# Mixture-of-experts kernel: weight maxima spread by one bf16 product, two experts without transposed results, one slot reordering moved

## The chip, the cores and the metric

The program runs on one core of a Trainium2 chip. Its engines are TensorE (PE, with its weight loads PEld), VectorE (DVE), ScalarE (ACT), GpSimd (POOL) and SyncE (SP, which issues transfers); each works through its own queue in order. The metric is the device time of one execution in microseconds (us).

## The reference

Attention over 4 batches of 768 tokens with 8 heads of 64, each query seeing the last 96 keys and 8 global ones, then a mixture of 8 experts of which each token uses two:

```
a = softmax(scale * q k^T + bias, masked);  x = a v           # x: 3072 tokens x 512
noisy = x @ w_gate + log1p(exp(x @ w_noise)) * noise
top2  = the two largest of 8 per token, weights = softmax of the two
for e in range(8):  out[tokens of e] += weight * (relu(x[tokens] @ w1[e]) @ w2[e])
```

Here w1[e] is 512 x 1024 and w2[e] is 1024 x 512, everything in float32.

## The kernel before

The first part (about 186 us) is attention, with gating and routing woven in. After it the experts run one after the other. An expert has a fixed number of slots, `CAPS`: 812 for the first three places, then 788, 776, 772, and 768 for places 6 and 7. The first two places hold experts 0 and 1; the other experts are put into places 2 to 7 by the number of their tokens (`rank`). The slots are split into a first part of 512 (four tiles of 128, `TA`) and the rest (300 down to 256, up to three tiles).

Products are done in three fp16 passes: every weight and activation is split into a high and a low half (`w1h`, `w1l`, `w2h`, `w2l`, `hh`, `hl`). To split the weights, each matrix needs one power-of-two scale, for which its largest magnitude must be known on all partitions. `scales` (line 156) does that, in six steps: four reductions `wmx` of 128x1024 on DVE (L162), then a PE transpose of the four columns (L166), a DVE maximum over them (L168) and a small diagonal (L170), and in the next step an fp32 product with ones (L173) and a maximum over its four columns (L175). It runs 16 times, twice for each expert. `step(e)` calls the next step of the preparation of expert e: these six, then eight `split`s, for W1 and then for W2. A table in the expert loop says how many steps follow which block of PE work; that order is what each engine's queue gets.

An expert's blocks on PE are:

- `up(e, 0, f)`, eight of twelve matmuls with 512 columns (L914), then `up(e, 1, f)`, eight on the rest of the slots. ACT writes `hh` (L924), DVE writes `hl` (L925).
- `down(e, t)`, four blocks of 24 matmuls with 512 columns (L947), one for each tile of the first part; the slots are the stationary operand, so the result has a slot on each partition and `put` writes it out (L931 on ACT, an adding indirect DMA on POOL, L932).
- `down_t(e, d)`, four blocks of 24 matmuls (L958) for the rest, with the weights stationary and 256 to 300 slots as columns. The result is transposed (`yt`, copied by ACT at L963 and DVE at L961), and `back` (L969) turns each tile round with four fp32 PE transposes before `put`. For all experts but the last this is done within the next expert's `up` blocks.

Between the blocks the next expert's token rows are gathered (POOL, L270), split (`ready`, `rest`: DVE L286 to L303, ACT L290) and transposed by DMA (`turn`). `permute(a, z)` (line 252) reorders the slot lists of places a to z-1 on DVE (L255, L257) and writes them as integers to `ids` (L258), which the gathers of these places read. `permute(2, 4)` stands after the sixth `up` block of expert 0's rest; `gather(2, ...)` follows in the third `up` block of expert 1.

Of the kernel before, what the change touches and what calls it, by code (L numbers as in the profile page):

```python
# [10 lines left out]
F32 = mybir.dt.float32  # L11
# [9 lines left out]
P = 128  # L21
# [15 lines left out]
def tile_local_global_attention_then_moe(  # L37
# [43 lines left out]
    def bank(tag, bufs):  # L81
        return psum.tile([P, 512], F32, name=tag, tag=tag, bufs=bufs)
# [26 lines left out]
    row = consts.tile([P, P], F16, name="row")  # L109
    col = consts.tile([P, E * (TT + 1)], F16, name="col")  # L110
    over = consts.tile([P, NT, E], F32, name="over")
    wmx = consts.tile([P, E, 2, 4], F32, name="wmx")
    wex = consts.tile([P, E, 2], F32, name="wex")
    wsc = consts.tile([P, E, 2], F32, name="wsc")
    fac = consts.tile([P, E], F32, name="fac")
    up2 = consts.tile([P, 2], F32, name="up2")
    one4 = consts.tile([4, P], F32, name="one4")
    noise_s = consts.tile([P, NT, E], F32, name="noise_s")
    wgn = consts.tile([P, KC, 32], F32, name="wgn")
    sel = consts.tile([P, 2 * E], F32, name="sel")  # L120
# [35 lines left out]
    def scales(e, x):  # L156

        m, c = wmx[:, e, x - 1], slice(x - 1, x)
        for i in range(4):
            t = raw[x, e, i // 2].rearrange("p k f -> p (k f)")  # L160
            n = t.shape[1] // 2
            nc.vector.tensor_reduce(m[:, i:i + 1], t[:, i % 2 * n:(i % 2 + 1) * n], op=OP.max, axis=AX.X,  # L162
                                    apply_absolute_value=True)
            yield
        ps = bank("sc", 3)
        nc.tensor.transpose(ps[:4, :P], m, ident)  # L166
        mc = small.tile([4, 1], F32, name="mc")
        nc.vector.tensor_reduce(mc, ps[:4, :P], op=OP.max, axis=AX.X)  # L168
        d4 = small.tile([4, 4], F32, name="d4")
        nc.vector.tensor_scalar(d4, ident[:4, :4], mc, TINY, op0=OP.mult, op1=OP.max)  # L170
        yield
        ps = bank("sc", 3)
        nc.tensor.matmul(ps[:, :4], one4, d4, start=True, stop=True)  # L173
        m1 = small.tile([P, 1], F32, name="m1")
        nc.vector.tensor_reduce(m1, ps[:, :4], op=OP.max, axis=AX.X)  # L175
        power(wex[:, e, c], m1, wsc[:, e, c])
        nc.vector.tensor_mul(wsc[:, e, c], wsc[:, e, c], up2[:, c])
        if x == 2:
            nc.vector.scalar_tensor_tensor(fac[:, e:e + 1], wex[:, e, 0:1], 2.0 ** -(1 + W1_UP + W2_UP),
                                           wex[:, e, 1:2], op0=OP.mult, op1=OP.mult)  # L180
        yield
# [20 lines left out]
    def weigh(e, a, z):  # L202
        c = l1[:, e, a:z]
        nc.vector.tensor_scalar(c.bitcast(I32), c.bitcast(I32), EXP, None, op0=OP.bitwise_and)
        nc.vector.scalar_tensor_tensor(yr[:, e, a:z], wv[:, e, a:z], fac[:, e:e + 1], c, op0=OP.mult, op1=OP.mult)
# [46 lines left out]
    def permute(a, z):  # L252
        for e in range(a, z):
            m = small.tile([P, TT, E], F32, name="m78")
            nc.vector.tensor_mul(m, flat[:, :, :TT].rearrange("p e t -> p t e"),  # L255
                                 pick[:, e, None, :].to_broadcast([P, TT, E]))
            nc.vector.tensor_reduce(flat2[:, e, :TT], m, op=OP.add, axis=AX.X)  # L257
        nc.vector.tensor_copy(ids[:, a:z, :TT], flat2[:, a:z, :TT])  # L258
# [237 lines left out]
    with ExitStack() as actx:  # L496
# [102 lines left out]

        def gate_consts():  # L600
            nc.vector.tensor_copy(ident16, ident)
            nc.vector.memset(one4, 1.0)
            nc.vector.memset(up2[:, 0:1], 2.0 ** (W1_UP - 1))
            nc.vector.memset(up2[:, 1:2], 2.0 ** (W2_UP - 1))
            nc.vector.memset(wgn, 0.0)
            nc.sync.dma_start(wgn[:, :, :2 * E], w_gn.rearrange("(k p) e -> p k e", p=P))
            nc.vector.tensor_add(sel, ident[:, 0:2 * E], ident[:, 32:32 + 2 * E])
            nc.vector.tensor_add(sel, sel, ident[:, 64:64 + 2 * E])
            nc.vector.tensor_add(sel, sel, ident[:, 96:96 + 2 * E])
# [287 lines left out]
    with ExitStack() as mctx:  # L897
# [42 lines left out]

        def down(e, t):
            ps = bank("av", 2)
            cols = slice(t * P, (t + 1) * P)
            n = 0
            for f in range(FC):
                for x, w in ((hh, w2h), (hh, w2l), (hl, w2h)):
                    nc.tensor.matmul(ps, x[0][:, f, cols], w[e % 2][:, f], start=n == 0, stop=n == 3 * FC - 1)  # L947
                    n += 1
            put(e, t, ps)

# [73 lines left out]
        for f in range(FC):  # L1024
            up(0, 1, f)
            if f in (0, 2, 4):
                rest(1, 1 + f // 2)
                turn(1, 1 + f // 2)
            if f in (0, 2):
                ready(1, 2 + f // 2)  # L1030
            if f in (0, 3):
                load_w()
            if f not in (0, 2):
                step(1)
            if f == 1:
                rank()
            if f == 5:
                permute(2, 4)
        ready(1, TA)
        for j in range(KC):  # L1040
            down_t(0, j)
            step(1)
            if j < TB:
                rest(1, TA + j)
                turn(1, TA + j)
                if j + 1 < TB:
                    ready(1, TA + j + 1)
        weigh(0, TA, TT)
        for e in range(1, E):
            last = e + 1 == E  # L1050
            for f in range(FC):
                up(e, 0, f)
                if f < tiles(e - 1) - TA:
                    back(e - 1, f)
                step(e, [0, 0, 0, 1, 0, 1, 2, 2][f])
                if f == 2 and not last:
                    for t in range(5):
                        gather(e + 1, t)
            weigh(e, 0, tiles(e))
            if e == 1:  # L1060
                permute(4, E)
                limits()
            for f in range(FC):
                up(e, 1, f)
                if f < 2:
                    step(e, 2)
                elif f < 6:
                    step(e + 1)
                if not last:
                    if f in (4, 6):  # L1070
                        ready(e + 1, f // 2 - 2)
                    if f in (5, 7):
                        rest(e + 1, f // 2 - 2)
                        turn(e + 1, f // 2 - 2)
                        if f // 2 + 3 < tiles(e + 1):
                            gather(e + 1, f // 2 + 3)
            steps = [(down, t) for t in range(TA)]
            steps_t = [(down_t, d) for d in range(KC)]
            for j, (f, t) in enumerate(steps_t + steps if last else steps + steps_t):
                f(e, t)  # L1080
                if not last:
                    if j < tiles(e + 1) - 2:
                        ready(e + 1, j + 2)
                    step(e + 1, [1, 3, 3, 3, 1, 1, 1, 1][j])
                    if j < tiles(e + 1) - 2:
                        rest(e + 1, j + 2)
                        turn(e + 1, j + 2)
                elif KC <= j < KC + tiles(e) - TA:
                    back(e, j - KC)


# [85 lines left out]
```

## Time and profile before

| | us |
|---|---|
| median of 3 runs | 738.0 (736.62 to 739.31) |
| span of the profiled execution | 738.1 |
| PE busy | 703.6 (95%) |
| DVE busy | 491.7 (67%) |
| ACT busy | 343.3 (47%) |
| POOL busy | 203.2 (28%) |

The page gives the profiled execution no time of its own beside its span, from the first to the last instruction. A matmul's printed length holds its way through the array and overlaps the next one, so the pace is read from start to start. In square brackets stands how long the engine was idle before an instruction, and what ended that.

### The profile page before, as it was taken

What the parts mean: (1) busy time and instruction counts of PE and PEld (TensorE: products, weight loads), DVE (VectorE), ACT (ScalarE), POOL (GpSimd) and SP (SyncE); (2) the same over time, 40 slices, a digit from 0 to 9 for tenths busy, and PEclk for the clock granted to TensorE, in tenths of its full rate; (3) what the DMA queues carried; (4) which work ended last, traced back from release to release, by engine and by line L of the source; (5) the groups of instructions that cost most, each with busy time, mean ns of one, the idle gap of its engine ahead of it and who ended that gap; (6) DMA issues with size and microseconds to landing.
All of it is one profiled execution on the core that took longest, in us unless ns stands there. A gap on an engine that the chain in (4) does not pass through costs nothing. (4 is left out here: it accounts for less than half of the span.)

```text
span 738.1 us, 16394 instructions
## 1 busy us (share of the span) xinstructions
PE 703.6 (95%) x6191; PEld 449.0 (61%) x6191; DVE 491.7 (67%) x1714; ACT 343.3 (47%) x740; POOL 203.2 (28%) x205
## 2 busy tenths in 40 slices
PE   7999988896999899999999999999999999999996
PEld 5888767675445665565646465655656475665762
DVE  6668996978688746873767386658837754873600
ACT  5887776666344424252443345243424434342511
POOL 2100185130337532224131504132240314121013
PEclk9999998999899999999999999999999999999999
DMA  7889794656608974395559538745954774472015
GB/s 222 254 275 286 231 316 133 224 187 244 243 6 161 215 151 135 106 199 88 168 101 177 106 121 143 143 105 153 172 113 149 113 169 92 105 111 28 1 18 74
DMA packets 105544, 111.43 MB, mean 151 GB/s; under 512 B 51332, under 2 KB 64340, under 8 KB 105456
## 3 DMA queue, kind: packets, MB, share of 16 engines
q1 hardware_dynamic: 93408, 83.89, 41.7%
q0 software_dynamic: 11504, 26.15, 20.2%
q8 instruction: 51, 0.84, 0.5%
q14 instruction: 37, 0.30, 0.1%
q10 hardware_dynamic: 544, 0.26, 0.1%
HBM read 71.22 MB, written 27.71 MB: 134 GB/s over the span
## 5 line engine op out<-in xcount | busy, mean ns | idle before, releaser
L932 POOL DMA_INDIRECT out_dram<-y,ids x54 | 85.7, 1587 | 210.1 <-ACT y L931 206.5
L914 PEld LDWEIGHTS <-w1h 128*128 128x128 f16 x1024 | 99.8, 98 | 64.5 <-issue 1.7
L914 PE MATMUL at<-xx,w1h 128*128 128x512 f16 (+5 forms) x512 | 124.7, 334 | 0.2 <-DVE hl L925 0.2
L914 PE MATMUL sc<-xx,w1h 128*128 128x512 f16 (+5 forms) x512 | 122.8, 330 | 0.0
L270 POOL DMA_INDIRECT xg<-xd,ids x54 | 55.4, 1026 | 159.4 <-DVE hl L925 86.0
L947 PE MATMUL av<-w2h,hh 128*128 128x512 f16 x256 | 97.1, 379 | 0.0
L947 PE MATMUL av<-w2l,hh 128*128 128x512 f16 x256 | 97.1, 379 | 0.0
L947 PE MATMUL av<-w2h,hl 128*128 128x512 f16 x256 | 97.1, 379 | 0.0
L682 ACT ACTIVATE a<-ns,mx 128x168 f32<-128x168 f32 (+1 forms) x192 | 69.6, 421 | 42.3 <-DVE mx L679 41.4
L914 PE MATMUL at<-xx,w1l 128*128 128x512 f16 (+5 forms) x256 | 85.3, 333 | 0.0
L914 PE MATMUL sc<-xx,w1l 128*128 128x512 f16 (+5 forms) x256 | 84.5, 330 | 0.0
L947 PEld LDWEIGHTS <-hh 128*128 128x128 f16 x512 | 49.5, 98 | 56.0
L925 DVE SCALAR_TENSOR_TENSOR hl<-sc,hh 128x512 f16<-128x512 f32 (+5 forms) x63 | 35.5, 564 | 66.4 <-ACT hh L924 66.4
L162 DVE TENSOR_REDUCE wmx<-raw 128x1 f32<-128x1024 f32 x64 | 76.5, 1207 | 0.0
L290 ACT ACTIVATE xp<-xg,up 128x512 f16<-128x512 f32 x48 | 34.6, 721 | 89.0 <-DVE up L288 75.7
L958 PE MATMUL av<-hl,w2h 128*128 128x300 f16 (+4 forms) x256 | 72.5, 283 | 2.5 <-DVE hl L925 2.5
L958 PE MATMUL av<-hh,w2h 128*128 128x300 f16 (+4 forms) x256 | 72.6, 284 | 1.0 <-DVE yt L961 1.0
L958 PE MATMUL av<-hh,w2l 128*128 128x300 f16 (+4 forms) x256 | 72.4, 283 | 0.0
L914 PEld LDWEIGHTS <-w1l 128*128 128x128 f16 x512 | 50.3, 98 | 35.6 <-issue 0.7
L924 ACT ACTIVATE hh<-at 128x512 f16<-128x512 f32 (+5 forms) x62 | 30.5, 491 | 88.7 <-PE at L914 88.7
L925 DVE SCALAR_TENSOR_TENSOR hl<-at,hh 128x512 f16<-128x512 f32 (+5 forms) x62 | 34.8, 560 | 51.7 <-ACT hh L924 51.7
L720 PE MATMUL av<-vs,at 128*64 128x65 f32 (+1 forms) x768 | 60.0, 233 | 0.0
(194 smaller groups left out, 1239.1 us busy)
## 6 DMA issues: line engine op xcount, KB each, us to landing
raw<-in_w SPq DMA_DIRECT2D x32, 1024.0 KB, 7.4
out_dram<-zero SPq DMA_DIRECT2D x14, 512.0 KB, 5.8
vs<-in_v SPq DMA_DIRECT2D x24, 260.0 KB, 3.9
xd<-xr SPq DMA_DIRECT2D x24, 256.0 KB, 6.4
qs<-in_q SPq DMA_DIRECT2D x23, 256.0 KB, 6.1
ks<-in_k SPq DMA_DIRECT2D x19, 272.0 KB, 6.6
vp<-in_v SPq DMA_DIRECT2D x20, 195.0 KB, 4.6
ks<-in_k SPq DMA_DIRECT2D x4, 464.0 KB, 4.8
```

The costliest lines, as they stand in the source:

```text
L162: nc.vector.tensor_reduce(m[:, i:i + 1], t[:, i % 2 * n:(i % 2 + 1) * n], op=OP.max, axis=AX.X, apply_absolute_value=True)
L270: nc.gpsimd.indirect_dma_start(out=xg[e, t], out_offset=None, in_=xd[:n], in_offset=bass.IndirectOffsetOnAxis(ap=rows(e, t), axis=0), boun ...
L290: nc.scalar.activation(y[:m, :Dm], x[:, :Dm], AF.Copy, scale=u)
L682: nc.scalar.activation(A[m][:, s * w:(s + 1) * w], ns[:, s, :w], AF.Exp, bias=mx[:, s:s + 1], scale=-1.0)
L720: nc.tensor.matmul(ps[y * Q:(y + 1) * Q, h % 4], w, t, start=id(x) in first, stop=id(x) in final, tile_position=(r, y * Q))
L914: nc.tensor.matmul(ps, w[e % 2][:, k, fs], xx[c][:, x + k, :z], start=n == 0, stop=n == 3 * KC - 1)
L924: nc.scalar.activation(hh[c][:, f, :z], ps, AF.Relu)
L925: nc.vector.scalar_tensor_tensor(hl[c][:, f, :z], ps, 0.0, hh[c][:, f, :z], op0=OP.max, op1=OP.subtract)
L932: ins = nc.gpsimd.indirect_dma_start(out=out, out_offset=bass.IndirectOffsetOnAxis(ap=rows(e, t), axis=0), in_=y, in_offset=None, bounds_c ...
L947: nc.tensor.matmul(ps, x[0][:, f, cols], w[e % 2][:, f], start=n == 0, stop=n == 3 * FC - 1)
L958: nc.tensor.matmul(ps, w[e % 2][:, f, cols], x[1][:, f, :z], start=n == 0, stop=n == 3 * FC - 1)
```

## The change

Three things. First, the spreading of the maxima: DVE takes the maximum over the four columns on each partition (with a fifth column that holds a tiny constant), keeps only its exponent, and multiplies the identity matrix by it into a bf16 diagonal `dm` of 128x128; one bf16 product with ones puts all 128 values on every partition, and DVE takes the maximum over them. The transpose and the fp32 product go. Second, an expert whose rest is a multiple of 128 (places 6 and 7) runs `down` for all six tiles, without `down_t`, `yt` and `back`; the table of steps for it has six entries instead of eight. Third, `permute(2, 4)` stands after expert 0's last `down_t` block and `weigh`.

```diff
-    wmx = consts.tile([P, E, 2, 4], F32, name="wmx")
+    wmx = consts.tile([P, E, 2, 5], F32, name="wmx")
-    one4 = consts.tile([4, P], F32, name="one4")
...
+        m1 = small.tile([P, 1], F32, name="m1")
+        nc.vector.tensor_reduce(m1, m, op=OP.max, axis=AX.X)
+        nc.vector.tensor_scalar(m1.bitcast(I32), m1.bitcast(I32), EXP, None, op0=OP.bitwise_and)
+        d = small.tile([P, P], BF, name="dm")
+        nc.vector.tensor_scalar(d, ident, m1, None, op0=OP.mult)
+        yield
         ps = bank("sc", 3)
-        nc.tensor.transpose(ps[:4, :P], m, ident)
-        mc = small.tile([4, 1], F32, name="mc")
-        nc.vector.tensor_reduce(mc, ps[:4, :P], op=OP.max, axis=AX.X)
-        d4 = small.tile([4, 4], F32, name="d4")
-        nc.vector.tensor_scalar(d4, ident[:4, :4], mc, TINY, op0=OP.mult, op1=OP.max)
-        yield
-        ps = bank("sc", 3)
-        nc.tensor.matmul(ps[:, :4], one4, d4, start=True, stop=True)
+        nc.tensor.matmul(ps[:, :P], ones, d, start=True, stop=True)
         m1 = small.tile([P, 1], F32, name="m1")
-        nc.vector.tensor_reduce(m1, ps[:, :4], op=OP.max, axis=AX.X)
+        nc.vector.tensor_reduce(m1, ps[:, :P], op=OP.max, axis=AX.X)
...
-            nc.vector.memset(one4, 1.0)
+            nc.vector.memset(wmx[:, :, :, 4:], TINY)
...
         def down(e, t):
             ps = bank("av", 2)
-            cols = slice(t * P, (t + 1) * P)
+            c = t // TA
+            cols = slice((t - c * TA) * P, (t - c * TA + 1) * P)
...
-                    nc.tensor.matmul(ps, x[0][:, f, cols], w[e % 2][:, f], start=n == 0, stop=n == 3 * FC - 1)
+                    nc.tensor.matmul(ps, x[c][:, f, cols], w[e % 2][:, f], start=n == 0, stop=n == 3 * FC - 1)
...
-            if f == 5:
-                permute(2, 4)
...
         weigh(0, TA, TT)
+        permute(2, 4)
...
-                if f < tiles(e - 1) - TA:
+                if f < tiles(e - 1) - TA and (CAPS[e - 1] - CA) % P:
                     back(e - 1, f)
...
+            straight = (CAPS[e] - CA) % P == 0
...
-            steps = [(down, t) for t in range(TA)]
-            steps_t = [(down_t, d) for d in range(KC)]
+            steps = [(down, t) for t in range(tiles(e) if straight else TA)]
+            steps_t = [] if straight else [(down_t, d) for d in range(KC)]
...
-                    step(e + 1, [1, 3, 3, 3, 1, 1, 1, 1][j])
+                    step(e + 1, ([1, 3, 3, 3, 2, 2] if straight else [1, 3, 3, 3, 1, 1, 1, 1])[j])
...
-                elif KC <= j < KC + tiles(e) - TA:
+                elif not straight and KC <= j < KC + tiles(e) - TA:
                     back(e, j - KC)
```

On PE, between the first three `down` blocks of expert 6, where W1 of expert 7 gets its scale, there stood:

```order
L947 LDWEIGHTS hl_4134
L947 MATMUL av<-w2h_4126,hl_4134 128x512
L166 MATMUL sc<-ident,wmx 4x128
L947 LDWEIGHTS hh_4132
...
L947 MATMUL av<-w2h_4126,hl_4134 128x512
L173 MATMUL sc<-d_8901,one_103 128x4
L947 LDWEIGHTS hh_4132
```

and now, at the second of the two points alone:

```order
L946 MATMUL av<-w2h_4123,hl_4131 128x512
L171 LDWEIGHTS ones
L171 MATMUL sc<-dm,ones 128x128
L946 LDWEIGHTS hh_4129
L946 MATMUL av<-w2h_4123,hh_4129 128x512
```

The transpose of `wmx` is gone, and the product with ones stands where the fp32 one stood. On DVE the two rows `mc` and `d` become three (`m` twice, `dm`) at the same place of its queue.

On DVE, at the end of expert 0's `up` blocks for its rest (`hl` of the sixth, seventh and eighth block; `m`, `flat` and `ids` are `permute`), there stood:

```order
L297 SCALAR_TENSOR_TENSOR xp<-xg,up,xp 128x512
L925 SCALAR_TENSOR_TENSOR hl_4135<-sc,hh_4133 128x300
L255 TENSOR_TENSOR m_4949<-flat,pick 128x56
L257 TENSOR_REDUCE flat_86<-m_4949 128x7
L255 TENSOR_TENSOR m_4952<-flat,pick 128x56
L257 TENSOR_REDUCE flat_86<-m_4952 128x7
L258 CAST ids<-flat_86 128x2x7
L925 SCALAR_TENSOR_TENSOR hl_4135<-at,hh_4133 128x300
L925 SCALAR_TENSOR_TENSOR hl_4135<-sc,hh_4133 128x300
```

and now, with the five rows behind the last `yt` copy, the fourth `wmx` and `weigh`:

```order
L923 SCALAR_TENSOR_TENSOR hl_4132<-sc,hh_4130 128x300
L923 SCALAR_TENSOR_TENSOR hl_4132<-at,hh_4130 128x300
L923 SCALAR_TENSOR_TENSOR hl_4132<-sc,hh_4130 128x300
...
L203 SCALAR_TENSOR_TENSOR yr<-wv,fac,l_79 128x3
L253 TENSOR_TENSOR m_5119<-flat,pick 128x56
L255 TENSOR_REDUCE flat_86<-m_5119 128x7
L253 TENSOR_TENSOR m_5122<-flat,pick 128x56
L255 TENSOR_REDUCE flat_86<-m_5122 128x7
L256 CAST ids<-flat_86 128x2x7
L923 SCALAR_TENSOR_TENSOR hl_4131<-at,hh_4129 128x512
```

The last two `hl` of expert 0 follow the one before them directly, and the five rows stand ahead of the first `hl` of expert 1.

On ACT, at the end of expert 6 and the start of expert 7, there stood:

```order
L216 ACTIVATE w1h_114<-raw,wsc 128x4x128 x3
L963 ACTIVATE yt<-av 128x256 x2
L924 ACTIVATE hh_4132<-at 128x512
L931 ACTIVATE y<-sc,yr 128x512
L924 ACTIVATE hh_4132<-sc 128x512
L931 ACTIVATE y<-lg,yr 128x512
```

and now:

```order
L214 ACTIVATE w1h_113<-raw,wsc 128x4x128 x3
L929 ACTIVATE y<-av,yr 128x512 x2
L922 ACTIVATE hh_4129<-at 128x512
L922 ACTIVATE hh_4129<-sc 128x512
```

The two results `y` of the rest come straight from the product's bank, ahead of expert 7's blocks.

## Rows read from the trace of the kernel before

**Rows 1.** The page's first line.
```profile
span 738.1 us, 16394 instructions
```
**Rows 2.** Stretch of experts 1 to 7: us, busy (instructions) by engine, granted clock, DMA.
```profile
265.10:730.60 465.50, 463.82 (x2817) 276.02 (x2815) 282.66 (x637) 178.82 (x319) 118.36 (x89) 1.00 0.58 117
```
**Rows 3.** Order of time, PE, expert 6's first `down` blocks: start, us, instruction.
```profile
639.38 0.27 PE L166 MATMUL sc<-ident,wmx 128*4 128x128 f32 x1
639.49 0.38 PE L947 MATMUL av<-w2h,hh 128*128 128x512 f16 x1
...
644.45 0.38 PE L947 MATMUL av<-w2h,hl 128*128 128x512 f16 x1
644.76 0.38 PE L173 MATMUL sc<-d,one 4*128 4x4 f32 x2
645.07 0.39 PE L947 MATMUL av<-w2h,hh 128*128 128x512 f16 x1
```
**Rows 4.** Order of time, PE, fp16 transposes of 128 columns.
```profile
229.68 0.62 PE L317 MATMUL sc<-ident,xp 128*128 128x128 f16 x8
230.14 0.61 PE L317 MATMUL lg<-ident,xp 128*128 128x128 f16 x8
```
**Rows 5.** DVE by line and shape: count, busy us, mean ns, idle before.
```profile
L168 DVE TENSOR_REDUCE mc<-sc 4x1 f32<-4x128 f32 x16 | 4.3, 270 | 0.4 <-PE sc L166 0.4
L170 DVE TENSOR_SCALAR d<-ident,mc 4x4 f32<-4x4 f32 x16 | 4.0, 253 | 0.6
L175 DVE TENSOR_REDUCE m<-sc 128x1 f32<-128x4 f32 x16 | 2.4, 152 | 0.0
...
L601 DVE CAST ident<-ident 128x128 f16<-128x128 f32 x1 | 0.2, 222 | 0.0
```
**Rows 6.** Who waited for whom, PE: total us, times, longest us.
```profile
PE av L958 <- DVE yt L961: 1.0, 3, 0.6
```
**Rows 7.** Order of time, expert 4's `down` blocks into `down_t`, DVE and PE.
```profile
521.57 2.08 DVE L221 SCALAR_TENSOR_TENSOR w1l<-raw,wsc,w1h 128x512 f16<-128x512 f32 x3 [1.45 <-ACT w1h L216]
...
533.38 0.27 PE L958 MATMUL av<-hh,w2h 128*128 128x264 f16 x1 [0.64 <-DVE yt L961]
```
**Rows 8.** Order of time, expert 3, POOL and DVE at a scale.
```profile
445.69 0.94 POOL L270 DMA_INDIRECT xg<-xd,ids  x1 [2.88 <-issue]
...
446.20 0.22 DVE L170 TENSOR_SCALAR d<-ident,mc 4x4 f32<-4x4 f32 x1
```
**Rows 9.** Order of time, around `permute(2, 4)`, all engines.
```profile
251.41 0.42 ACT L924 ACTIVATE hh<-sc 128x300 f16<-128x300 f32 x1
...
251.51 0.29 PE L958 MATMUL av<-hl,w2h 128*128 128x300 f16 x1 [0.83 <-DVE hl L925]
...
253.72 0.41 PE L958 MATMUL av<-hl,w2h 128*128 128x300 f16 x1 [1.66 <-DVE hl L925]
```
**Rows 10.** Stretches, columns as in rows 2 (a POOL column too), granted clock third from the end.
```profile
179.60:185.30 5.70, 3.25 (x70) 2.65 (x70) 4.62 (x19) 3.34 (x8) 0.00 (x0) 1.00 0.27 102
...
250.20:253.60 3.40, 1.02 (x7) 0.52 (x6) 3.26 (x10) 2.25 (x5) 3.32 (x3) 1.00 0.38 62
253.60:257.00 3.40, 3.28 (x14) 1.98 (x14) 3.33 (x9) 1.03 (x2) 3.24 (x3) 0.50 1.00 373
```
**Rows 11.** Order of time, PE, expert 6's `down_t` blocks and a `back`.
```profile
655.44 0.27 PE L958 MATMUL av<-hh,w2h 128*128 128x256 f16 x1
...
665.92 0.59 PE L914 MATMUL at<-xx,w1h 128*128 128x512 f16 x2
...
668.51 0.60 PE L969 MATMUL sc<-ident,yt 128*128 128x128 f32 x4
668.95 0.59 PE L914 MATMUL sc<-xx,w1h 128*128 128x512 f16 x2
```
**Rows 12.** Order of time, attention, W2 of expert 0: PE and DVE.
```profile
129.75 0.27 PE L166 MATMUL sc<-ident,wmx 128*4 128x128 f32 x1 [2.02 <-DVE sli L450]
...
132.40 0.16 DVE L725 TENSOR_SCALAR den<-av 128x4 f32<-128x4 f32 x1 [0.85 <-PE av L720]
```

## The prediction

> **What bounds the kernel now.** I read the page's head for the span, 738.1 us [rows 1], then the busy time by stretch. In the stretch of experts 1 to 7, 63% of the span, PE is busy 463.82 of 465.50 us at a granted clock of 1.00, DVE 282.66, ACT 178.82 [rows 2]. The reader is to see that PE has no room there: a PE instruction that goes shortens the span by its own pace, unless another engine then ends the block. Third, PE in order of time at the instructions that go [rows 3, 11], for their pace from start to start. Fourth, the list of who PE waited for [rows 6] and the places of its longest waits [rows 7, 9, 12], since what PE saves ahead of a wait on another engine comes back as a longer wait.
>
> The runs have a median of 738.0 us, 0.1 under the profiled span; I work from 738.1.
>
> **The maxima, PE's part.** Expert matmuls with 512 columns follow each other by 0.216 us: from 639.49 to 644.45 there are 23 of them in 4.96 us [rows 3]. The transpose takes 639.38 to 639.49, 0.11 us. The fp32 product takes more: from the start of the last matmul before it, 644.45, to that of the first one after it, 645.07, are 0.62 us, where 0.216 would pass without it, so 0.40 us. Together 0.51 us go for each scale.
>
> The new product has 128 columns of 16 bits with a weight load ahead of it. Nothing in the trace is just that. The nearest is eight transposes of 128 fp16 columns, each with a weight load of its own: 229.68 to 230.14, 0.057 us each [rows 4]. A bound above is 0.40, what the fp32 product costs; below it is nothing. I take 0.06, the row that agrees with it in columns and width. That leaves 0.45 saved at each scale. There are 14 within the experts' work (two each for experts 1 to 7): 6.3 us. The two of expert 0 lie in attention and come below.
>
> **The maxima, DVE's part.** Before: L168 0.27, L170 0.25, L175 0.15, sum 0.67 us. After: a maximum over five columns and a mask, each about like L175 (0.15), the diagonal, nearest a cast of 128x128 fp32 to 16 bits (L601, 0.22), and a maximum over 128 values in PSUM, nearest L168 with as many for each partition (0.27): 0.79 us [rows 5]. So DVE has 0.12 us more for each scale; its own waits for the transpose go.
>
> In most places that is hidden behind PE. It is not in the `down` blocks, where DVE and ACT work in turns: DVE waits for ACT's `w1h` 1.45 us before its three `w1l` in expert 4, ACT having waited for DVE's row scales before. At the end of that chain stands DVE's `yt` copy, and PE waits for its bank 0.64 us [rows 7]. There are three such waits, 1.0 us in all [rows 6]. In these three experts PE comes 0.45 us earlier and the chain ends 0.12 us later, so the wait can grow by up to 0.57 us: 1.7 us in all, or nothing if the chain starts from PE's `down` results after all. I take 1.3, near the upper end, because the wait that is shown in front of the chain's longest step is for ACT and not for PE. Left of this part: 6.3 - 1.3 = 5.0 us.
>
> **The slots of places 2 and 3.** At 251.51 PE waits 0.83 us for the sixth `hl` of expert 0, and at 253.72 another 1.66 us for the seventh, which on DVE stands behind the five rows of `permute` [rows 9]. The first wait stays, since that `hl` stands ahead of `permute` before and after. The second goes, down to what the eighth `hl` needs: ACT has its `hh` at 251.41 + 0.42 = 251.83 us [rows 9], and DVE follows; I leave 0.1 for that. So 1.55 us.
>
> In the 3.4 us of these two waits PE was busy 1.02 us, and the granted clock then fell to 0.50, the 1.2 GHz level, for 3.4 us, in which 14 matmuls started [rows 10]; at 2.4 GHz they take half of that, so the fall cost some 1.6 us. With the second wait gone PE is idle about 1 us there. In attention PE was busy 3.25 of 5.70 us from 179.60 on and the clock stayed at 1.00 all that time [rows 10]. So I take it that the clock holds, 1.6 us; the other end is nothing. Sum 3.15 us.
>
> What the step issues where it now stands: five DVE instructions, about 1.3 us, no transfer of its own. Behind them on DVE waits the first `hl` of expert 1, which nobody needs before that expert's `down`, and its bank is wanted two blocks of 2.6 us later. The gathers of place 2 stand on POOL behind three `put`s of expert 0, which come with expert 1's first three blocks, so `ids` is in time. Cost nothing; if the cover were gone, at most the 1.3 us. SP's queue keeps its order.
>
> **The two straight experts.** `down_t` in expert 6 takes 655.44 to 665.92, 10.48 us for 96 matmuls [rows 11]. Instead there are 48 with 512 columns at 0.216, 10.35. Each `back` takes four fp32 transposes, 668.51 to 668.95, 0.44 us [rows 11], and there are two for each expert. So 0.13 + 0.88 = 1.0 us, twice: 2.0 us. DVE and ACT lose the `yt` copies. The two `put`s come earlier, and the last instructions of the program, a `down` block, its `y` and its transfer, are of the same kind and size as before.
>
> **Attention.** At 129.75 PE has waited 2.02 us at the transpose, whose PSUM bank DVE still reads, and DVE in turn waits 0.85 us for PE's `av` at 132.40 [rows 12]. Without the transpose PE goes on, but DVE has little idle time there, so the gain is what DVE waited, 0.85, less its 0.12. Ends: the whole 2.02 plus 0.9 for the PE time of the two scales, and a loss of 0.5 if DVE's added work falls where it sets the pace. I take 0.7.
>
> **Sum.** 5.0 + 3.15 + 2.0 + 0.7 = 10.85, so 738.1 - 10.85 = 727.2 us.
>
> **Rivals.**
> 1. *Nothing is given back.* If the `yt` chain hangs on PE's results, its 1.3 us are saved, and attention may give up to 2 us more: 724 us. For it: ACT's `y` in the same blocks does wait for PE. Against it: the three waits are there now.
> 2. *The clock falls again.* After the wait that stays at 251.51, or at the longer `yt` wait of expert 4 (0.64 + 0.57 = 1.2 us). Each costs 1.6: 728.8 or 730.4 us. Against it: the stretch from 179.60.
> 3. *POOL holds up the diagonal.* At 446.20 the small diagonal ran 0.22 us inside a POOL gather of 0.94 us [rows 8], unhindered. The 128x128 one may not be: if it waits out such a gather, 0.7 us more come into the chain in the `down` blocks of six experts, 4.2 us, 731.4 us. The Trainium skill, page "SBUF — State Buffer", section "Who interferes with whom", says that a `tensor_scalar` in a two-port mode and a GpSimd instruction shut each other out for a whole instruction, whoever comes first. By that rule the 0.22 us row should have ended only with the gather, so the trace does not bear it out for the 4x4 form; no run here shows the 128x128 form.
> 4. *The product isn't cheap.* If the bf16 product costs PE the 0.40 us of the fp32 one, 14 x 0.34 = 4.8 us go: 732.0 us. Then the change would not do what it says. Against it: the fp16 transposes.
> 5. *Slower.* Rival 3, and in each of those `down` blocks the longer wait takes the clock down too, 1.6 us each. With n of them 731.4 + 1.6 n; from five on (739.4) it is slower than before, with six 741.0 us. Against it: no wait for `yt` has done that so far.
>
> **How the numbers follow.** Forecast 55% (own range 725.5 to 729), rival 1 17%, rival 2 14%, rival 3 7%, rival 4 4%, rival 5 3%. The range leaves out rivals 4 and 5, most of 3, and what runs scatter: 723.0 to 731.0 us. A difference of 0.3%, 2.2 us, is about what a measurement tells from no change. All cases but rival 5 are more than that below 738.0; for mishaps in two parts at once I allow some: faster 0.93, same 0.04, slower 0.03.
>
> **What would show it.** Right: L173's successor 0.06 us long from start to start, with no matmul behind it late; the PE wait for `hl` near 251 us once, under 1.2 us, and no half clock after it; no `down_t` in the last two experts, whose time from the first `down` block on is 1 us shorter; PE's waits for `yt` longer, 2.3 us in three places. Wrong: a wait of PE for `dm`, a `dm` of over 0.5 us beside POOL, a half clock in the experts, or attention longer than 186 us.

## The result, and the profile after

The changed kernel takes 730.06 us (median of four runs, 729.51 to 730.3) where the kernel before takes 738.57 in the same set (736.62 to 739.31): ratio 0.9878, 95% interval 0.9846 to 0.9910, so 8.5 us less. The forecast was 10.85 less, 727.2 us, with a range of 723.0 to 731.0. Two further sets of runs, on chips 14 and 12 (the chip of the first set is not on record), gave 0.9842 (0.9813 to 0.9871) and 0.9876 (0.9852 to 0.9901), 11.5 and 9.2 us less. What is the same in all of them, and what differs, is the matter of the experiments.

One thing on the scale first: a run's time lies 1.7 to 1.8 us above its span (730.3 against 728.5 for the changed kernel's profiled run). The forecast set before's span, 738.1, against the medians, so its profiled execution was one of the longer ones.

The page's first line of after, which answers to [rows 1]:

```profile
span 728.5 us, 16104 instructions
```

The stretch of experts 1 to 7 in after, from the first `up` of expert 1 to the last matmul (us, then busy time and instructions of PE, PEld, DVE, ACT, POOL, granted clock, DMA share, GB/s), against [rows 2]:

```profile
262.25:720.87 458.62, 455.54 (x2678) 261.85 (x2676) 285.34 (x653) 178.47 (x315) 118.37 (x89) 1.00 0.57 120
```

The stretch of [rows 2] is 0.27 us wider than these bounds; between the same two points before's trace has 465.23 us (265.15 to 730.38), of which PE is busy 463.55. So 465.2 have become 458.6, 6.6 less; PE's busy time fell by 8.0, and 1.4 us came back as waiting. PE is still what is busy nearly always, at the same clock.

The new product on PE in after, expert 6's first `down` blocks in order of time (start, us), against [rows 3]:

```profile
637.76 0.38 PE L946 MATMUL av<-w2h,hl 128*128 128x512 f16 x1
637.98 0.22 PE L171 MATMUL sc<-dm,ones 128*128 128x128 bf16 x1
638.03 0.38 PE L946 MATMUL av<-w2h,hh 128*128 128x512 f16 x1
```

Read from start to start, not by the printed 0.22: the product takes 637.98 to 638.03, and the matmul ahead of it keeps its 0.216. So it costs 0.056 us, what the fp16 transposes of [rows 4] cost.

DVE's new steps in after, by line and shape (count | busy us, mean ns | idle before), against [rows 5]:

```profile
L168 DVE TENSOR_SCALAR dm<-ident,m 128x128 bf16<-128x128 f32 x16 | 5.1, 317 | 0.6
L173 DVE TENSOR_REDUCE m<-sc 128x1 f32<-128x128 f32 x16 | 4.5, 280 | 0.0
L166 DVE TENSOR_SCALAR m<-m 128x1 int32<-128x1 int32 x16 | 2.5, 153 | 0.5
L165 DVE TENSOR_REDUCE m<-wmx 128x1 f32<-128x5 f32 x16 | 2.4, 149 | 0.0
```

Together 0.90 us for each scale, 0.11 more than the 0.79 forecast; `dm` is the one that was sized too small, 0.32 in the mean and not 0.22 (0.29 where nothing holds it, up to 0.40 beside a gather, of which more below).

Who PE waited for in after (total us, times, longest), against [rows 6]; of the page's list only what touches the change:

```profile
PE sc L171 <- DVE mx L677: 2.6, 2, 2.0
PE av L957 <- DVE yt L960: 2.3, 3, 1.2
PE av L957 <- DVE hl L923: 0.8, 1, 0.8
```

The three waits for `yt` have grown from 1.0 to 2.3 us, as forecast to the tenth. Of the two waits for `hl` at expert 0's `down_t` one is left, against [rows 9, 10], PE in order of time and then the 3.4 us behind it:

```profile
251.91 0.29 PE L957 MATMUL av<-hl,w2h 128*128 128x300 f16 x1 [0.84 <-DVE hl L923]
```

```profile
252.00:255.40 3.40, 3.40 (x27) 2.49 (x27) 3.29 (x7) 1.87 (x4) 3.32 (x3) 1.00 0.55 158
```

27 matmuls in 3.4 us at a clock of 1.00, where before's trace shows 14 at 0.50.

The reader gets most from one pair of numbers: the time from expert 0's first `down_t` block to the last matmul. It is 730.38 - 248.47 = 481.9 us in before's trace and 720.87 - 248.86 = 472.0 in after's, 9.9 us less. The 248 us ahead of it became 0.4 longer, where 0.7 less was forecast for attention; 1.6 of the 9.9 are a stretch at half clock that only this trace of before has, as the next experiment shows.

### The profile page after: what moved, and what is told of

Same layout as the page of the kernel before. It is cut to its first block, busy times and chain, and to the rows that moved or that the text cites. A ratio compares the mean times of both kernels' runs of the same rounds, so it can differ in the third digit from the quotient of the medians.

```text
span 728.5 us, 16104 instructions
## 1 busy us (share of the span) xinstructions
PE 694.5 (95%) x6047; PEld 435.0 (60%) x6047; DVE 493.8 (68%) x1726; ACT 343.1 (47%) x736; POOL 203.9 (28%) x205
## 5 line engine op out<-in xcount | busy, mean ns | idle before, releaser
L946 PE MATMUL av<-w2h,hh 128*128 128x512 f16 x288 | 109.2, 379 | 0.0
L946 PE MATMUL av<-w2h,hl 128*128 128x512 f16 x288 | 109.2, 379 | 0.0
L946 PE MATMUL av<-w2l,hh 128*128 128x512 f16 x288 | 109.2, 379 | 0.0
L946 PEld LDWEIGHTS <-hh 128*128 128x128 f16 x576 | 56.0, 98 | 66.2 <-issue 0.9
L718 PE MATMUL av<-vp,at 104*64 104x65 f32 (+1 forms) x640 | 55.2, 233 | 2.6 <-ACT at L693 1.8
L957 PE MATMUL av<-hh,w2h 128*128 128x300 f16 (+3 forms) x192 | 54.5, 284 | 2.3 <-DVE yt L960 2.3
L929 ACT ACTIVATE y<-av,yr 128x512 f32<-128x512 f32 x36 | 24.7, 685 | 67.1 <-PE av L946 31.9
```

The costliest lines, as they stand in the source:

```text
L718: nc.tensor.matmul(ps[y * Q:(y + 1) * Q, h % 4], w, t, start=id(x) in first, stop=id(x) in final, tile_position=(r, y * Q))
L929: nc.scalar.activation(y, ps, AF.Copy, scale=yr[:m, e, t:t + 1])
L946: nc.tensor.matmul(ps, x[c][:, f, cols], w[e % 2][:, f], start=n == 0, stop=n == 3 * FC - 1)
L957: nc.tensor.matmul(ps, w[e % 2][:, f, cols], x[1][:, f, :z], start=n == 0, stop=n == 3 * FC - 1)
```

## The experiments

In what follows "the rest" is that time from the first `down_t` block to the last matmul, and "the head" what lies before it.

**The kernel before again.** 

> The kernel before, unchanged, traced a second time. In the trace of after, the attention part ended 1.8 us later than before's (first up block of expert 0 at 188.13 us, not 186.30), with four short PE gaps at 161 to 164 us in which no instruction is waited for. Theory A (that part scatters from run to run, by when transfers land): the first up block starts somewhere between 184 and 189 us here, and from expert 0's first down_t block to the end the times are those of the first trace within 0.2 us. Theory B (the change makes attention later): 186.3 within 0.3 us. Ratio 1.000 within 0.002 in both.

Measured: ratio 1.0006 (0.9981 to 1.003), head 247.2 us (first `up` block at 186.31), rest 727.55 - 247.23 = 480.3. The head agrees with the first trace to 1.2 us; the first `up` block stands where B had it, within A's range too, and the traces of the changed kernel told of below, 182.50 us in one, speak against B. The rest does not agree with the first trace: it is 1.6 us shorter than the 481.9, and the reason is in one place. Around `permute(2, 4)` in this second trace (columns as above, both waits in the first row):

```profile
250.20:252.50 2.30, 0.56 (x4) 0.30 (x4) 2.16 (x8) 1.01 (x3) 2.29 (x2) 1.00 0.21 33
252.50:255.90 3.40, 3.40 (x27) 2.61 (x27) 3.33 (x8) 1.03 (x2) 3.23 (x4) 1.00 0.99 361
```

The waits are those of [rows 9], 0.83 and 1.67 us, but the clock stays at 1.00 behind them. Two more kernels have both waits in their traces (below, the spreading alone and the straight experts alone), and neither shows the half clock. So of four traces with these waits one has it, the one that the forecast was made from.

**The three parts alone.** The new spreading, the move of `permute`, and the straight experts, each put alone into the kernel before; the edits are the parts of the diff.

> The kernel before with the new spreading of the maxima alone. Theory A (PE saves 0.47 us for each scale, and three waits for yt take 1.3 us of it back): from expert 1's first up block to the last matmul 4.6 us less than before's 465.2, the three waits for yt 2.3 us in all; attention gains nothing, since DVE sets its pace: 733.5 us in before's span of 738.1, ratio 0.994. Rival (the yt waits grew by another part of the change): 5.9 us less, waits for yt 1.0 us as before, ratio 0.992.

> The kernel before with permute(2, 4) alone moved behind expert 0's last down_t block. Theory A (wait of 1.55 us and half clock of 1.6 us go together): down_t of expert 0 takes 13.4 us instead of 16.7, no granted clock under 1.00 between 250 and 260 us, no new wait in expert 1: 3.3 us less, ratio 0.9955. Rival (the half clock comes from the wait that stays at 251.5 us): 1.6 us less, clock at 0.50 for 3.4 us after 252, ratio 0.998.

> The kernel before with the two experts of 768 slots alone run without transposed results. Theory A (four fp32 transposes of 0.44 us go twice for each expert, and 0.13 us by 48 matmuls with 512 columns instead of 96 with 256): 2.0 us less, all of it behind 634 us, ratio 0.9973. Rival (expert 6's table of six steps lets DVE's splits fall behind, so expert 7's first blocks wait): 1 us less or none, with a PE wait for w1l or hl in expert 7's up blocks.

| | ratio (95%) to before | rest, us | less than 480.3 |
|---|---|---|---|
| spreading alone | 0.9910 (0.9877 to 0.9943) | 721.78 - 246.03 = 475.7 | 4.6 |
| `permute` alone | 0.9964 (0.9942 to 0.9985) | 728.00 - 248.61 = 479.4 | 0.9 |
| straight alone | 0.9969 (0.9945 to 0.9994) | 722.17 - 243.83 = 478.3 | 2.0 |
| all three | 0.9878 (0.9846 to 0.9910) | 472.0 | 8.3 |

The spreading gives 4.6 us in the rest, as its theory A had it, and its trace has the longer waits while the two others keep the old ones; spreading, `permute`, straight in this order:

```profile
PE av L956 <- DVE yt L959: 2.3, 3, 1.2
```

```profile
PE av L958 <- DVE yt L961: 1.0, 3, 0.6
```

```profile
PE av L959 <- DVE yt L962: 1.0, 3, 0.6
```

So the growth belongs to the spreading. The straight experts give their 2.0 us, all of it from expert 6's first `down` block on, as expected. `permute` alone missed its expectation of 3.3: the second wait is gone, but there was no half clock to gain in the program that it is measured against, and in its trace PE also stands still at the first matmul of expert 1, for nothing that the profile shows:

```profile
262.77 0.59 PE L914 MATMUL at<-xx,w1h 128*128 128x512 f16 x2 [0.61 <-issue]
```

That gap makes 0.8 us from start to start, and its cause isn't shown; without it `permute` gives 1.7, and 4.6 + 1.7 + 2.0 = 8.3, the rest's whole gain. Expert 0's `down_t` tells the same without the gap: 13.4 us in after (262.25 - 248.86), 15.1 in before's second trace (262.32 - 247.23).

**The changed kernel again, twice.** 

> The changed kernel, unchanged, traced a second time. From expert 0's first down_t block to the last matmul 472.0 us as in its first trace, within 0.2. Theory A (the four PE gaps at 161 to 164 us, in which nothing is waited for, came of that one execution): none of them here, and first down_t block before 246 us. Theory B (they belong to the changed program, whose instructions stand elsewhere): again 1 us or more of such gaps between 155 and 170 us, and first down_t block near 248.9.

> The changed kernel, unchanged, timed beside the two others of this set. From the first down_t block to the last matmul 472.0 us within 0.1. Its median lay 8.5 us under before's in one set of runs and 11.5 in another; Theory A (8.3 us of it are the experts', fixed, and the rest is the attention part's, which differs between chips): 8 to 12 us again, and the trace differs from the other two of after only ahead of the first down_t block. Rival (the first set was short of runs, four each, and 11.5 is the value): 11 to 12 us.

Measured: 724.9 us against 736.38 (0.9842), and 730.12 against 739.27 (0.9876). The rest is 716.24 - 244.21 = 472.0 and 721.46 - 249.41 = 472.1: three traces within 0.1. All that differs is the head, 244.2 against 248.9 and 249.4. The two long ones have gaps at the same place, which but for one the profile puts down to no wait, PE in order of time, the first trace and the third:

```profile
162.04 0.25 PE L718 MATMUL av<-vp,at 40*64 40x65 f32 x1 [0.41 <-issue]
162.80 0.25 PE L718 MATMUL av<-vp,at 40*64 40x65 f32 x1 [0.42 <-DMA raw<-in_w]
163.55 0.47 PE L670 MATMUL sc<-ks,qs 64*64 64x168 f32 x2 [0.35 <-issue]
164.27 1.13 PE L670 MATMUL sc<-ks,qs 64*64 64x168 f32 x11 [0.26 <-issue]
```

```profile
162.25 0.25 PE L718 MATMUL av<-vp,at 40*64 40x65 f32 x1 [0.39 <-issue]
162.98 0.25 PE L718 MATMUL av<-vs,at 64*64 64x65 f32 x1 [0.42 <-issue]
163.72 0.52 PE L670 MATMUL sc<-ks,qs 64*64 64x168 f32 x4 [0.21 <-issue]
164.49 0.86 PE L670 MATMUL sc<-ks,qs 64*64 64x168 f32 x8 [0.25 <-issue]
```

The trace of the second set has none, though it is the same program; the two other kernels of the third set (told of below) both have them. So B is wrong, since the same program is free of them; A's numbers came, but with the three traces of the third set the gaps are more than the matter of one execution. Of the second expectation A holds: 9.2 us lie in its range and not in the rival's. That they go with the chip would fit: all three traces on chip 12 have them, and none of the nine on chips 3, 14 and 1. It isn't shown, since each chip was traced in one set only, and before's first trace, whose chip isn't on record, has none. Behind the gaps the clock is at half for some 7 us in these two traces (163.7 to 170.5 in the first), where the second set's trace has 1.00. An estimate from these rows: 1.4 us of gaps and half of some 6.8 us at half clock are 4.8 us, about what the heads differ by. But it isn't fixed to the gaps: of the two other kernels with them one has 3.4 us of half clock behind them and one none. Nor does the head scatter with the chip alone: on chip 3 the three traces with before's attention part have heads of 243.8, 247.2 and 248.6 us, and 29 runs of before there go from 733.8 to 739.9. What PE lacked in the gaps isn't shown; the queues were full (share 0.99, 345 GB/s from 156.96 to 163.79), but in the trace without gaps they were as full (0.96, 331 GB/s from 156.50 to 163.30). It stays open.

**Attention with the old spreading.** The changed kernel, with the old steps for expert 0 alone:

```diff
+        if e == 0:
+            nc.tensor.transpose(ps[:4, :P], m[:, :4], ident)
+            ...
+            nc.tensor.matmul(ps[:, :4], one4, d4, start=True, stop=True)
+        else:
             m1 = small.tile([P, 1], F32, name="m1")
```

> The changed kernel with the spreading of before (transpose, two maxima, fp32 product) for expert 0 alone, whose two scales lie in the attention part. Theory A (DVE has no idle time there, so what PE saves at the transpose it waits later for its bank): the wait of 2.0 us stands again at the transpose and not at the product, the median is that of the changed kernel within 1 us. Theory B (the two scales' savings count there too, 0.85 us of DVE idle time among them): 1 to 3 us longer than the changed kernel.

Measured: 733.7 us (729.55 to 734.57) beside 730.12 (728.96 to 731.07) for the changed kernel on the same chip, 3.6 longer; the intervals of the two ratios overlap (0.9880 to 0.9941 and 0.9852 to 0.9901), and two of its six runs, 729.55 and 730.52, lie among the changed kernel's. The head is 2.8 us longer (252.19 against 249.41), with as much half clock in both (27.3 us) and the gaps in both. The long wait does stand again at the transpose, here and in the changed kernel:

```profile
129.39 0.27 PE L167 MATMUL sc<-ident,wmx 128*4 128x128 f32 x1 [2.04 <-DVE sli L462]
```

```profile
131.58 0.23 PE L171 MATMUL sc<-dm,ones 128*128 128x128 bf16 x1 [2.05 <-DVE mx L677]
```

So the wait has only moved, as A says, and yet the time is nearer to B. Of the 3.6 us 0.6 aren't attention's: the rest is 472.7 us here, since PE stands still at expert 1's first matmul as it did with `permute` alone:

```profile
266.13 0.59 PE L927 MATMUL at<-xx,w1h 128*128 128x512 f16 x2 [0.41 <-issue]
```

Over a scatter of 5 us between runs I count what is left as 0 to 3 us, by a way that no single row shows; whether it is more than the 0.7 forecast isn't shown.

**`dm` written twice.**

```diff
         nc.vector.tensor_scalar(d, ident, m1, None, op0=OP.mult)
+        nc.vector.tensor_scalar(d, ident, m1, None, op0=OP.mult)
```

> The changed kernel with the diagonal dm written twice by the same instruction, 0.32 us more on DVE for each scale. Theory A (DVE's added time reaches PE only where DVE ends a block): each of the three waits for yt 0.3 us longer (expert 1's perhaps in its wait for dm), expert 6's wait for dm 0.1 us, nothing at the seven scales within up blocks: 1.1 us more than 472.0, not 14 x 0.32 = 4.5. Rival (the yt chain starts from PE's results in these blocks): 0.45 us at most, all of it in waits for dm.

Measured: rest 716.62 - 243.96 = 472.7, 0.65 more, between the two. The wait for `dm` in expert 1 grew by 0.32 (0.65 to 0.97) and took 0.22 off the `yt` wait behind it; in experts 3 and 4 the `yt` waits grew by 0.13 and 0.11, expert 6's product came 0.18 late; at the seven `up` places nothing. So within the rest DVE's added time reaches PE only in the `down` blocks, and a third of it there: the chain isn't DVE's alone. Ahead of the rest it reached PE whole, at the one scale within expert 0's blocks, where the wait for `hl` grew from 0.41 to 0.73:

```profile
240.90 0.41 PE L913 MATMUL at<-xx,w1h 128*128 128x300 f16 x2 [0.73 <-DVE hl L924]
```

**What the chain is.** Expert 4's `down` blocks in after, DVE and then ACT, in order of time (idle before and its end in brackets):

```profile
520.22 0.15 DVE L286 TENSOR_SCALAR up<-l 128x1 int32<-128x1 int32 x1
521.83 2.08 DVE L219 SCALAR_TENSOR_TENSOR w1l<-raw,wsc,w1h 128x512 f16<-128x512 f32 x3 [1.45 <-ACT w1h L214]
...
527.75 0.41 DVE L960 COPY yt<-av 128x264 f32<-128x264 f32 x1
```

```profile
520.46 0.72 ACT L288 ACTIVATE xp<-xg,up 128x512 f16<-128x512 f32 x1 [0.85 <-DVE up L286]
521.09 1.93 ACT L214 ACTIVATE w1h<-raw,wsc 128x512 f16<-128x512 f32 x3
```

The reader is to see a circle: ACT's `xp` waits for DVE's row scales `up`, `w1h` stands behind `xp`, DVE's `w1l` waits 1.45 us for `w1h`, and the next tile's `up` stands behind `w1l`. Once round is 5.43 us (516.40 to 521.83 for `w1l`), a block of PE is 5.18. The next four kernels give the steps in another order.

**The steps given later.** Table 1, 3, 3, 3, 0, 1, 2, 1 for experts 1 to 5, and the same with 2, 3, 2, 3 in front:

```diff
-  step(e + 1, ([1, 3, 3, 3, 2, 2] if straight else [1, 3, 3, 3, 1, 1, 1, 1])[j])
+  step(e + 1, ([1, 3, 3, 3, 2, 2] if straight else [1, 3, 3, 3, 0, 1, 2, 1])[j])
```

> The changed kernel with the steps of the next expert's preparation given as 1, 3, 3, 3, 0, 1, 2, 1 instead of 1, 3, 3, 3, 1, 1, 1, 1 in experts 1 to 5: the fifth split stands on DVE and ACT behind the yt copy of the second down_t block instead of ahead of it. Theory A (PE's three waits for yt come of what DVE has queued ahead of that copy, not of PE's own results): the copy ends 2 us earlier, all three waits (2.3 us) go, no new one over 0.3 us, 2.7 us less than after's 472.0 from the first down_t block to the last matmul. Rival (the chain of ACT and DVE is late as a whole, and only changes place): waits of 1 us or more for the fourth yt copy or for w1l in the next expert's up blocks, less than 1 us gained.

> As later_splits, with the maxima of W1 one step earlier too: 2, 3, 2, 3, 0, 1, 2, 1 (2, 3, 2, 3, 2, 2 in expert 6), so that dm stands on DVE a whole down block ahead of the product. Theory A: expert 1's wait of 0.64 us for dm goes as well, 3.5 us less than after's 472.0. Rival (the maxima then wait for W1's transfer, and DVE stands idle): the dm wait stays or DVE waits for raw, gain as later_splits or less.

Measured: rest 471.3 and 512.4 us, medians 725.91 and 763.97 (ratio 1.0370, 1.0340 to 1.0401). Both expectations rest on a wrong reading of the table: the four maxima of W1 are taken in the `up` blocks before, so the first entry is `dm`, and the fifth isn't a split but W2's first maximum. The first kernel took that maximum (1.20 us) from ahead of the `yt` copy, and only 0.25 us of it reached each of the three waits (2.3 to 1.5 us together); in expert 4 DVE then waited 0.79 us for ACT's `xpb`. The second put `dm` and its product into one step, with no block of PE's between them. PE then waits in six places, 28.2 us in all, and at each the clock falls within the wait or as it ends; expert 4, PE and then a stretch:

```profile
521.13 0.27 PE L171 MATMUL sc<-dm,ones 128*128 128x128 bf16 x1 [4.74 <-DVE dm L168]
```

```profile
521.40:524.80 3.40, 3.40 (x9) 1.22 (x8) 2.58 (x10) 0.00 (x0) 1.59 (x1) 0.50 0.51 53
```

So it is the block of PE's between the two that hides `dm`.

**The calls turned round.** `step` ahead of `ready` in all eight blocks:

```diff
+  step(e + 1, ...)
   if j < tiles(e + 1) - 2:
       ready(e + 1, j + 2)
-  step(e + 1, ...)
```

> The changed kernel with the calls in the expert loop in another order: after each down and down_t block step(e + 1, ...) stands ahead of ready(e + 1, j + 2), not behind it. ACT's w1h then no longer stands behind its xp, which waits for DVE's row scales. Theory A (the three waits for yt and expert 1's for dm end a chain in which ACT and DVE wait for each other once in every block, 5.43 us a block where PE needs 5.18): from the trace of after, DVE's block becomes 2.08 for w1l, 1.0 for row scales, 0.8 waiting for ACT's xp, 1.05 for xp and weights, 4.9 us in all; all waits for yt (2.3 us) and for dm (0.65) go, from the first down_t block to the last matmul 468.5 us instead of 472.0, median 3.5 us under the changed kernel's on this chip. Rival (the chain is only turned round): DVE waits for xp what it waited for w1h, waits for yt of 1 us or more, or for xx in the next expert's up blocks; less than 1 us gained.

Measured: rest 725.66 - 248.56 = 477.1 us, 5.1 more; median 735.12 beside 730.12. The wait for `dm` is gone, but the `yt` copies of both engines are late:

```profile
PE av L957 <- ACT yt L962: 4.2, 5, 1.0
PE av L957 <- DVE yt L960: 3.1, 2, 1.8
```

The rival was right: the circle is turned round, not opened.

**The two halves of a split parted.** ACT's `w1h` ahead of `ready`, DVE's `w1l` behind it, in the four `down` blocks alone:

```diff
+  if j < KC:
+      held.append([])
+      step(e + 1, n)
   if j < tiles(e + 1) - 2:
       ready(e + 1, j + 2)
+  if j < KC:
+      for g in held.pop():
+          g()
+  else:
+      step(e + 1, n)
...
+        if held:
+            held[0].append(tail)
+        else:
+            tail()
```

The last four lines stand in `split`; `tail` issues `w1l` and, behind each fourth one, the next weight transfer.

> The changed kernel with each split's two halves parted in the four down blocks: ACT's w1h is issued ahead of the next tile's row scales (ready), DVE's w1l behind them; the maxima's dm goes ahead of ready too; the down_t blocks keep their order. Theory A (PE's waits for yt and for dm end a chain in which, once a block, DVE waits 1.45 us for w1h, which stands on ACT behind xp, which waits for DVE's row scales): w1h needs nothing of that block, xp runs beside DVE's w1l, DVE has 4.1 us of work in a block of 5.18 and waits for neither; waits for yt (2.3 us) and for dm (0.65) under 0.3 us together, from the first down_t block to the last matmul 468.5 us instead of 472.0. Rival (the yt copies are late for what stands on DVE and ACT within the down_t blocks, as turning all eight calls round showed 7.3 us of yt waits): waits for yt stay at 1 us or more, 471 us or more. The attention part differs between chips by 5 us, so the stretch decides, not the median.

Measured: rest 712.11 - 243.63 = 468.5 us, as expected, median 722.32 against 736.17 (0.9816, 0.9785 to 0.9847). No wait for `yt` or `dm` is left in its list; what is left of PE's waits in the rest are those for `hl`, 0.84 us in expert 0 and 0.18 in expert 1 (the 0.42 in the second line lie ahead of the rest):

```profile
PE av L968 <- DVE hl L934: 0.8, 1, 0.8
PE at L923 <- DVE hl L934: 0.6, 2, 0.4
```

Expert 4's `down` blocks there, DVE and ACT:

```profile
507.75 2.07 DVE L222 SCALAR_TENSOR_TENSOR w1l<-raw,wsc,w1h 128x512 f16<-128x512 f32 x3 [0.48 <-ACT w1h L216]
...
512.88 2.07 DVE L222 SCALAR_TENSOR_TENSOR w1l<-raw,wsc,w1h 128x512 f16<-128x512 f32 x3 [1.15 <-ACT w1h L216]
```

```profile
511.55 0.69 ACT L940 ACTIVATE y<-av,yr 128x512 f32<-128x512 f32 x1 [2.00 <-PE av L957]
512.13 1.94 ACT L216 ACTIVATE w1h<-raw,wsc 128x512 f16<-128x512 f32 x3
513.97 0.71 ACT L299 ACTIVATE xp<-xg,up 128x512 f16<-128x512 f32 x1
```

DVE still waits for `w1h`, against what I expected, but `w1h` now starts from PE's own block (ACT's `y` waits for `av`), and from one `w1l` to the next are 5.13 us. This is the version that beats both kernels: 3.5 us less than the changed kernel in the rest (the medians of the two are from different chips). `dm` stands ahead of `ready` here too, so the 0.65 us of expert 1's wait for `dm` are not the parted halves' alone.

## Why the prediction was right, and where its sum was off

The median fell as forecast and inside the range, 0.9 us under its upper end. The terms that could be checked in fixed stretches came out (8.55 us forecast, 8.3 measured); the other two, 2.3 us of the clock and of attention, do not show in the first set's medians. By its steps:

- *The maxima, PE's part.* Right. A scale saves 0.47 us (forecast 0.45) at every place but two; the product costs 0.056 (0.06). Of the 14 scales one, W1 of expert 1, lies in expert 0's blocks, ahead of the rest, where a new wait for `hl` of 0.41 us at 245.81 takes it back. The other place is expert 1's `down` blocks, next.
- *The maxima, DVE's part.* Right in kind and size: three waits for `yt`, 1.0 to 2.3 us, 1.3 given back as forecast, and the kernel with the halves parted shows the chain that was named, DVE and ACT in turns, to be the cause. Not named was expert 1, where PE already waited 0.48 us for the small diagonal; it now waits 0.64 for `dm`, and the scale taken there gives 0.22. With both, 4.6 us came of the 5.0.

```profile
308.24 0.22 PE L171 MATMUL sc<-dm,ones 128*128 128x128 bf16 x1 [0.64 <-DVE dm L168]
```

- *The slots of places 2 and 3.* The wait went: 1.7 us (forecast 1.55). The clock term, 1.6, was right for the execution that it was read from, and only there: the three other traces with the same waits show no half clock behind them. Against a median it should have counted with a chance. This is the term of the sum that was mis-sized. That the clock would hold once the second wait is gone came true, but the row that stood for it was badly chosen: the stretch of [rows 10] from 179.60, at 1.00 with PE busy 3.25 of 5.70 us, ends where the clock falls in the same trace:

```profile
185.30:192.20 6.90, 6.40 (x29) 2.94 (x26) 5.28 (x28) 1.37 (x4) 3.43 (x5) 0.51 0.88 303
```

- *The two straight experts.* 2.0 forecast, 2.0 measured.
- *Attention.* 0.7 forecast. What was measured goes from 0.4 us longer (the first pair of traces) to some 3 shorter (the second set: 11.5 us less, of which 8.3 in the rest, or up to 9.9 where before's clock falls). The step's premise, that PE goes on without the transpose, failed: the wait of 2.0 us stands now at the product, for the same kind of bank.

Together: 4.6 + 1.7 + 2.0 = 8.3 us are fixed. To them come 0 or 1.6 by before's clock, and about 0 to 3 in the head, by the set of runs. The first set of runs, 8.5, lies at the lower end of that, 11.5 at the upper. Of the signs that the forecast gave for being wrong two came, without turning it: PE waits for `dm` (0.64 us, in expert 1), and attention is longer than 186 us in two of three traces of the changed kernel (first `up` block at 188.1 and 188.5 us, in the other at 182.5).

Of the rivals none came in at its price. Rival 1 is ruled out by the growth of the `yt` waits. Rival 2: the clock stayed at 1.00 behind the wait that is left at 251.91 and behind expert 4's `yt` wait, now 1.2 us. Rival 4: the product costs 0.056 us. Rival 5 needs rival 3's price and a half clock behind the waits for `yt`, and neither came. Rival 3 has a true mechanism under a price that was too high. Expert 4's scale in after, POOL and DVE in order of time:

```profile
507.02 0.93 POOL L268 DMA_INDIRECT xg<-xd,ids  x1 [2.86 <-issue]
507.58 0.39 DVE L168 TENSOR_SCALAR dm<-ident,m 128x128 bf16<-128x128 f32 x1
```

The gather ends at 507.95 and `dm` at 507.97. In experts 1 to 4 of after's first and third trace, eight cases, `dm` ends 0.02 to 0.03 us behind a gather that it began 0.56 to 0.60 us into, and takes 0.37 to 0.40 us; where no gather is under way it takes 0.29. But where it begins within the first 0.1 us of a gather, as in the `up` blocks of experts 3 to 6, it takes 0.29 too and ends long before the gather. And where it begins late, as in expert 0's blocks, it takes 0.29 as well and ends 0.15 us behind the gather:

```profile
223.90 1.02 POOL L268 DMA_INDIRECT xg<-xd,ids  x1 [0.30 <-issue]
224.79 0.29 DVE L168 TENSOR_SCALAR dm<-ident,m 128x128 bf16<-128x128 f32 x1
```

Before's own trace had the effect already, for the 4x4 form; the forecast read it from the one place at 446.20 [rows 8], where there is none. Of the four small diagonals in the `down` blocks of experts 1 to 4 two took 0.41 and 0.38 us, both begun 0.53 us into a gather, and two 0.22, begun 0.51 and 0.49 us into one. The first of them:

```profile
310.57 0.97 POOL L270 DMA_INDIRECT xg<-xd,ids  x1 [2.93 <-issue]
311.10 0.41 DVE L170 TENSOR_SCALAR d<-ident,mc 4x4 f32<-4x4 f32 x1
```

So the rule that the prediction cites from the Trainium skill (page "SBUF — State Buffer", section "Who interferes with whom") agrees with the starts 0.53 to 0.60 us into a gather, in both forms, and not with those before or behind, so not with a whole instruction; no row shows whether either form ran in the two-port mode that the rule asks for. The price is 0.1 us a scale in four experts, not the 0.7 of rival 3: `dm` begins past the middle of the gather, and little of it is left to wait for.

## What to carry to other kernels

A term that is read from one profiled execution is a sample: in the experts the waits of PE for DVE came back within 0.02 us in every trace of one kernel, but a half clock behind such a wait came in one of four, and goes into a sum as a chance. Where two engines hand work to each other once in every block, time their circle against the block of the engine that sets the end; if it is longer, work taken from or added to one of them shows only in part (here a fifth and a third), and what helped here was to issue first what needs nothing of this block. And where the ends of one kernel scatter, compare a stretch that begins behind the scatter.

## What the runs showed of the hardware that was not expected

The gaps of PE in attention, four within 3 us and all but one with nothing waited for, stand between 161 and 168 us in all three traces of the third set and in the first of after, and in none of the ten other traces, one of them of the same program. A wait of PE of 1.67 us was followed by half clock in one of four traces, and one of 1.77 us for `yt`, with the calls turned round, was not; each of the six waits of 3.6 to 5.8 us in the kernel with `dm` and its product in one step was. And `dm` was held to the end of a gather that it began 0.56 to 0.60 us into, as above, 0.1 us each.
